# A fused attention and MLP kernel: roots moved ahead of most of a batch's loads, two small loads moved to another queue, and later loads issued earlier in the unit

## Chip, cores, metric

One core of one Trainium2 chip. The metric is the device time of one execution in microseconds (us). Most executions of this kernel lie within 1% of their median; a run over 1.5% above the fastest of the same kernel is marked slow, and only fast runs are compared. In the profile PE is TensorE's matmuls, PEld its weight loads, DVE is VectorE, ACT is ScalarE, POOL is GpSimd and SP is SyncE, which issues hardware DMAs.

## The reference, cut to what matters

```python
# B, H, S, D = 4, 8, 768, 64; 24 chunks of 32 queries; 8 memory rows per head
for c in range(24):                                   # window: 16 left, 32 own, 8 right
    k_full = concat([mem_k, k[:, :, l_start:r_end]])
    v_full = concat([mem_v, v[:, :, l_start:r_end]])
    a = softmax(q_c @ k_full.T / 8)
    attn[:, :, chunk] = a @ v_full
x   = attn.transpose(0, 2, 1, 3).reshape(4, 768, 512)
xn  = (x - mean(x)) / sqrt(var(x) + 1e-6) * g
out = x + relu(xn @ w_ch1) @ w_ch2                    # 512 -> 2048 -> 512, all float32
```

## The kernel before

The 3072 rows of x are 24 tiles of 128 rows. Three tiles make a **unit**; unit u has an up stage (16 groups of four 384-wide products, steps 0 to 15) and a down stage (steps 16 to 27). The attention of the next units, the loads of the next batches and the small work of the other engines are hung on these steps by a hand-made plan: `at(u, step, function, arguments)` emits the function behind that step of unit u. Each engine carries out its list in order.

```python
def load_block(b, blk, which):          # keys or queries of 256 rows, software queue (POOL)
    s = pick(st, ("b", b, blk, which))
    for par in range(2):
        nc.gpsimd.dma_start(out=s[:, 512 * par : 512 * par + 512], in_=dram((k, q)[which], ...))

def load_v(b, g):                       # values of one window pair, software queue (POOL)
    nc.gpsimd.dma_start(out=V[b % 2][lo:hi, g, :, 0:64], in_=dram(v, ...))

def v_mem(b, g0, g1, eng):              # copies the mem values into V, 16 bit, SBUF to SBUF
    copy(eng, V[b % 2][96:W, g0:g1, ...], memv16[96:W, b, ...])

def mix(b, blk, which, eng):            # a raw block to 16-bit layout, SBUF to SBUF
    copy(eng, free(iv_tile, 0, [[64, 2], [128, 8], [1, 64]]), st_tile)

def root(b, t):                         # 1 / sqrt(var) of a tile: two instructions on POOL
    nc.gpsimd.tensor_scalar(out=veps[t % 3], in0=sq[t], ...)
    nc.gpsimd.tensor_tensor(out=rstd[(NT * b + t) % 9], in0=veps[t % 3], in1=mhalf, op=ALU.pow)

def turn_x(b, t):                       # x tile transposed for the up stage
    i = NT * b + t
    if i // 3 >= XU:                    # XU = 2: from unit 2 on a DMA does it
        nc.sync.dma_start_transpose(out=dst, in_=xn[i % 4])
        return
    ...                                 # units 0 and 1: four TensorE transposes, one DVE copy

def finish(t, p):                       # result of a tile; needs the root
    nc.vector.scalar_tensor_tensor(out=o, in0=p, scalar=rstd[t % 9], in1=xs[t % 9],
                                   op0=ALU.mult, op1=ALU.add)
    nc.sync.dma_start(out=out[...], in_=o)
```

The parts of the plan that the change touches (cuts marked with ...):

```python
def attend(i, s0, s1, u):
    ...
    at(u, s1 + (3 if i // 3 < XU else 2), turn_x, b, t)
    at(u, s1 + 2, stats, b, t)                        # sum of squares, ACT
    if i < 6:
        at(1, i % 3, root, b, t)
    else:
        at(i // 3 - 1, 20 + i % 3, root, b, t)
for t in range(3):
    at(0, 13 + t, stats, 0, t)
    at(0, 19 + t, root, 0, t)                         # roots of unit 0
...
order = [(load_pair, (0,))] + [(load_v, (g,)) for g in range(4)]      # batch 1's loads
order += [(load_pair, (1,)), (mem_cols, (pool,)), (load_v, (4,)), (load_v, (5,))]
order += [(load_pair, (2,))] + [(load_v, (g,)) for g in range(6, 12)]
for n, (fn, args) in enumerate(order):
    at(0, 14 + n // 2, fn, *((1,) + args))
...
for b in (2, 3):
    u = 2 * b - 1
    w = u - 1
    for blk in range(3):
        at(w - 1, 23 + blk, load_pair, b, blk)
    at(w, 0, mem_cols, b, pool)
    for g in range(NG):
        at(w, 1 + g // 2, load_v, b, g)
    for i in range(3):
        at(w, 8 + i, v_mem, b, 4 * i, 4 * i + 4, pool)
    for blk in range(3):
        for which in range(2):
            at(w, (3, 9, 18)[blk] + which, mix, b, blk, which, dve)
            at(w, (7, 18, 23)[blk] + 3 * which, cross, b, blk, which)   # DMA transposes
    ...
```

The softmax here doesn't subtract the row's maximum and nothing guards it: scores larger than these inputs give would overflow.

Of the kernel before, what the change touches and what calls it, by code (L numbers as in the profile page):

```python
# [15 lines left out]
def kernel(  # L16
# [12 lines left out]
    nc = tc.nc  # L29
# [53 lines left out]
    turn = {"att": 0, "mm": 0}  # L83
# [6 lines left out]
    def dram(t, offset, pattern):  # L90
        return bass.AP(tensor=t.tensor, offset=offset, ap=[list(p) for p in pattern])

    def free(ap, off, pattern, parts=None):
        p = list(ap.ap[0]) if parts is None else [ap.ap[0][0], parts]
        return bass.AP(tensor=ap.tensor, offset=ap.offset + off, ap=[p] + [list(x) for x in pattern])

    def as16(t):
        return t.bitcast(FP16)

    def copy(eng, out, in_):  # L100
        if eng is nc.scalar:
            eng.copy(out=out, in_=in_)  # L102
        else:
            eng.tensor_copy(out=out, in_=in_)  # L104
# [45 lines left out]
    def mem_keys():  # L150
        p = slot("att")
        pv = as16(p[:, 0, :])
        for half in range(2):
            for par in range(2):
                nc.tensor.matmul(
                    out=pv[64 * par : 64 * par + 64, 128 * half : 128 * half + 128],
                    lhsT=memk16[:, half, :], rhs=identity,
                    is_transpose=True, start=True, stop=True, tile_position=(0, 64 * par),
                )
        for par in range(2):  # L160
            rows = slice(64 * par, 64 * par + 64)
            nc.scalar.copy(
                out=memKT[rows, :, :, :].rearrange("p b j m -> p b (j m)"),
                in_=free(pv[rows, :], 32 * par, [[64, 4], [1, 32]]),
            )
# [31 lines left out]
    def window(b, blk, banks, k0, eng):  # L197

        for half in ((0, 1) if eng is dve else (1, 0)):
            key_piece(b, banks[half], 4 * blk + k0, *PIECES[k0], eng, half)  # L200
# [32 lines left out]

    block_slot = {}

    def quarter_q(b, blk, half, banks):

        for n, eng in ((0, dve), (1, act)):
            copy(eng, free(QR[b % 2], 1024 * blk + 512 * n + 64 * half, [[128, 4], [1, 64]]),
                 free(banks[n], 64 * half, [[128, 4], [1, 64]]))  # L240

    def part_q(b, blk, half, pv, eng):
        copy(eng, free(QR[b % 2], 1024 * blk + 64 * half, [[128, 8], [1, 64]]),
# [181 lines left out]
    def warm(n, m=512, p=None):  # L425
        p = mm[3] if p is None else p
        for _ in range(n):
            nc.tensor.matmul(out=p[:, 0:m], lhsT=zero[:, 0:128], rhs=zero[:, 0:m], start=True, stop=True)


    raws = ((osb[0], osb[1]), (osb[2], xs[4]))
    for which, eng in ((0, nc.sync), (1, nc.scalar)):
        for par in range(2):
            eng.dma_start(
                out=raws[which][par],
                in_=dram((k, q)[which], 4 * par * HS, [[512, 32], [HS, 4], [1, 512]]),
            )
# [3 lines left out]
            out=xs[5 + b][96:W, :], in_=dram(mem_v, b * 4096, [[64, 8], [512, 8], [1, 64]])  # L441
        )

    nc.sync.dma_start(out=memkf, in_=dram(mem_k, 0, [[64, 128], [128 * 64, 2], [1, 64]]))
    nc.sync.dma_start(out=grow, in_=dram(moe_g_ln, 0, [[512, 1], [1, 512]]))
    load_mem_v(0, nc.sync)

    PAIR = 1.0 / 128 + 15.0 / 2**20
# [61 lines left out]
    load_w2(2)  # L510
    load_w2(3)

    warm(6)
    K0 = [as16(mm[0]), as16(mm[1])]
    Q0 = [as16(mm[2]), as16(mm[3])]
    mix_raw(0, raws[0], 0, dve)
    mix_raw(0, raws[0], 1, act)
    mem_keys()
    transpose_block(0, 0, 0, K0)
    mix_raw(1, raws[1], 0, dve)  # L520
    mix_raw(1, raws[1], 1, act)
    window(0, 0, K0, 0, dve)
    window(0, 0, K0, 1, act)
    transpose_block(0, 0, 1, Q0)
    mem_cols(0, dve)
    quarter_q(0, 0, 0, Q0)
    mem_vals(0)
    scores(0, 0)
    soften(0, 0, 0)
    soften(0, 0, 1)  # L530
    window(0, 0, K0, 2, dve)
    p = slot("att")
    nc.tensor.matmul(out=p[:, 0, :], lhsT=gone, rhs=grow, start=True, stop=True)  # L533
    copy(act, gb, p[:, 0, :])
    window(0, 0, K0, 3, act)
    quarter_q(0, 0, 1, Q0)
    mix(0, 1, 0, dve)
    v_mem(0, 0, 2, dve)
    total(cnt[:, 0:1], 16, 128)
    count_v(0, 0, 0)  # L540
    values(0, 0)
    transpose_block(0, 1, 0, K0)
    norm(0, 0)
    window(0, 1, K0, 0, dve)
    key_right(0, 3, dve)
    window(0, 1, K0, 1, act)
    warm(1, 512, mm[2])
    turn_x(0, 0)
    scores(0, 1)
    soften(0, 1, 0)  # L550
    soften(0, 1, 1)
    v_mem(0, 2, 4, dve)
    turn["mm"] = 2
    up_tile(0, 0, 0, act)
    window(0, 1, K0, 2, dve)
    window(0, 1, K0, 3, act)
    key_left(0, 4, dve)
    values(0, 1)
    norm(0, 1)
    warm(1, 512, mm[2])  # L560
    mix(0, 1, 1, dve)
    up_tile(0, 1, 0, act)
    turn_x(0, 1)
    Q1 = [as16(slot("mm")) for _ in range(2)]
    transpose_block(0, 1, 1, Q1)
    quarter_q(0, 1, 0, Q1)
    up_tile(0, 0, 1, act)
    scores(0, 2)
    soften(0, 2, 0)
    soften(0, 2, 1)  # L570
    quarter_q(0, 1, 1, Q1)
    v_mem(0, 4, 6, dve)
    up_tile(0, 1, 1, dve)
    up_tile(0, 2, 0, dve)
# [2 lines left out]
    up_tile(0, 2, 1, act)  # L577
    mix(0, 2, 0, dve)
    up_tile(0, 3, 0, act)
    up_tile(0, 3, 1, dve)  # L580
    turn_x(0, 2)
    mix(0, 2, 1, dve)
    total(cnt[:, 1:2], 0, 80)
    total(cnt[:, 2:3], 96, W)
# [6 lines left out]
    def attend(i, s0, s1, u):  # L591

        b, t = divmod(i, NT)
        at(u, s0, scores, b, t)
        at(u, s0, soften, b, t, 0)
        at(u, s0 + 1, soften, b, t, 1)
        at(u, s1, values, b, t)
        at(u, s1 + 1, norm, b, t)
        at(u, s1 + (3 if i // 3 < XU else 2), turn_x, b, t)
        at(u, s1 + 2, stats, b, t)  # L600
        if i < 6:
            at(1, i % 3, root, b, t)
        else:
            at(i // 3 - 1, 20 + i % 3, root, b, t)

    at(0, 12, turn_keys, 0, 2)
    at(0, 13, more_keys, 0, 2)
    at(0, 14, turn_queries, 0, 2)
    for t in range(3):
        at(0, 13 + t, stats, 0, t)  # L610
        at(0, 19 + t, root, 0, t)
    attend(3, 15, 18, 0)
    at(0, 18, count_v, 0, 1, NG - 1)
    attend(4, 18, 21, 0)
# [13 lines left out]
    order = [(load_pair, (0,))] + [(load_v, (g,)) for g in range(4)]  # L628
    order += [(load_pair, (1,)), (mem_cols, (pool,)), (load_v, (4,)), (load_v, (5,))]
    order += [(load_pair, (2,))] + [(load_v, (g,)) for g in range(6, 12)]  # L630
    for n, (fn, args) in enumerate(order):
        at(0, 14 + n // 2, fn, *((1,) + args))
    at(0, 25, count_v, 1, 0, 0)
# [23 lines left out]
    for b in (2, 3):  # L657
        u = 2 * b - 1
        w = u - 1
        for blk in range(3):  # L660
            at(w - 1, 23 + blk, load_pair, b, blk)
        at(w, 0, mem_cols, b, pool)
        for g in range(NG):
            at(w, 1 + g // 2, load_v, b, g)
        for i in range(3):
            at(w, 8 + i, v_mem, b, 4 * i, 4 * i + 4, pool)
        for blk in range(3):
            for which in range(2):
                at(w, (3, 9, 18)[blk] + which, mix, b, blk, which, dve)
                at(w, (7, 18, 23)[blk] + 3 * which, cross, b, blk, which)  # L670
        at(w, 18, spread, b, 0, dve, act)
        at(w, 27, spread, b, 1, dve, act)
        at(u, 9, spread, b, 2, dve, act)
        attend(6 * b, 2, 7, u)
        attend(6 * b + 1, 7, 13, u)
        attend(6 * b + 2, 13, 18, u)
# [54 lines left out]
```

## Time and profile before

| | before |
|---|---|
| time, median of 3 runs | 231.66 us (230.74 to 231.68) |
| the profiled run | 233.87 us, marked slow; span 232.1 us, mean clock 0.985 |
| PE idle in front of unit 1 | 4.48 + 1.03 us |
| half clock | 6.83 us, from 54.86 on |

The profile that the prediction reads is that of a run 2.2 us above the median, and it was the only one of this kernel. The prediction shows its main lines. The waits of PE complete the picture (who waited for whom; us in total, times, longest): behind the hole in front of unit 1 little is left.

```profile
PE mm L364 <- DVE xT L351: 4.5, 1, 4.5
...
PE mm L364 <- DVE osb L399: 1.0, 1, 1.0
PE mm L364 <- DVE rT L358: 1.0, 1, 1.0
...
PE mm L364 <- DMA xT<-xn: 0.4, 1, 0.4
```

Two lines of the same run's timeline (start, length, engine, operation) become important later. The prediction did not look at them:

```profile
100.21 7.50 POOL L104 COPY V<-memv 8x2560 f16<-8x2560 f16 x3
103.00 2.54 DVE L104 COPY iv<-st 128x1024 f16<-128x1024 f16 x1
```

The same DVE copy takes 0.42 us elsewhere in this trace (at 88.58, 109.00 and others). Beside POOL's copy of the mem values it took 2.54.

### The profile page before, as it was taken

How to read it: one execution, taken by the hardware profiler on the slowest of the kernel's cores; microseconds unless marked ns; L12 is line 12 of the kernel's file. 1: busy time of each engine (PE TensorE's matmuls, PEld its weight loads, DVE VectorE, ACT ScalarE, POOL GpSimd, SP SyncE). 2: the span in 40 equal slices, each digit the busy share in tenths (PEclk: the TensorE clock that was granted, in tenths of full speed). 3: DMA queues.
4: the chain of work that ended last, by engine and by line, in shares of the span. 5: the costliest groups of instructions: out<-in, count | busy, mean ns of one | idle time of the engine just before them, and what ended most of it. 6: DMA issues, size and time to landing. Idle time of an engine off the chain costs nothing.

```text
span 232.1 us, 4947 instructions
## 1 busy us (share of the span) xinstructions
PE 214.6 (92%) x1942; PEld 131.1 (56%) x1942; DVE 134.8 (58%) x324; ACT 103.9 (45%) x219; POOL 111.0 (48%) x172
## 2 busy tenths in 40 slices
PE   4789989955999999999999999997999999999993
PEld 1557985523675557644674466544664566456552
DVE  2867675546486736899685268733674366433221
ACT  2644557620577227742584047702791176104200
POOL 8967755799311668599211965579112002100000
PEclk9999999997699999999999999999999999999999
DMA  6999999999501699998911799999913203211012
GB/s 196 183 198 195 197 192 206 161 158 174 66 3 23 75 190 219 143 150 106 246 32 23 141 212 141 141 110 165 205 24 84 85 15 48 67 47 45 3 45 90
DMA packets 72857, 27.85 MB, mean 120 GB/s; under 512 B 60929, under 2 KB 68865, under 8 KB 72834
## 3 DMA queue, kind: packets, MB, share of 16 engines
q0 software_dynamic: 45632, 14.56, 65.0%
q1 hardware_dynamic: 26914, 12.46, 27.9%
q10 hardware_dynamic: 288, 0.52, 0.8%
q8 instruction: 15, 0.25, 0.5%
q14 instruction: 8, 0.07, 0.1%
HBM read 30.28 MB, written 6.29 MB: 158 GB/s over the span
## 4 chain that ended last, share of the span: by engine, by line
PE 81%; DMA 6%; DVE 4%; POOL 3%; ACT 2%; issue 1%; SPq 1%; DVEq 0%; ACTq 0%
PE mm L364 32%; PE mm L390 29%; PE att L277 6%; PE mm L375 5%; DMA rawk<-iv 5%; PE att L298 4%; DMA memkf<-in_mem_k_dram 2%; PE mm L212 2%; POOL V L128 2%; PE mm L412 2%; PE att L212 1%; POOL st L120 1%; DVE xs L306 1%; PE att L533 1%; POOL rstd L333 1%
## 5 line engine op out<-in xcount | busy, mean ns | idle before, releaser
L364 PE MATMUL mm<-xT,w1c 128*128 128x384 f16 x448 | 80.7, 333 | 7.1 <-DVE xT L351 4.5
L390 PE MATMUL mm<-w2c,rT 128*128 128x512 f16 x368 | 82.6, 379 | 0.0
L364 PEld LDWEIGHTS <-w1c 128*128 128x128 f16 x448 | 49.4, 115 | 31.4 <-issue 9.6
L390 PEld LDWEIGHTS <-rT 128*128 128x128 f16 x368 | 34.9, 98 | 40.0
L358 DVE TENSOR_SCALAR rT<-mm 128x384 f16<-128x384 f32 (+1 forms) x61 | 34.3, 569 | 26.2 <-PE mm L364 22.6
L356 ACT ACTIVATE rT<-mm 128x384 f16<-128x384 f32 (+1 forms) x63 | 31.6, 505 | 37.2 <-PE mm L364 19.2
L128 POOL DMA_DIRECT2D V<-in_v_dram x48 | 39.0, 818 | 16.1 <-DMA V<-in_v_dram 4.0
L287 ACT ACTIVATE AT<-att,band 104x512 f16<-104x512 f32 x48 | 31.4, 686 | 28.5 <-PE att L277 28.5
L399 DVE SCALAR_TENSOR_TENSOR osb<-mm,rstd,xs 128x512 f32<-128x512 f32 x23 | 17.2, 751 | 36.5 <-PE mm L390 29.4
L329 POOL TENSOR_SCALAR veps<-sq 128x1 f32<-128x1 f32 x24 | 5.9, 246 | 61.4 <-ACT junk L323 47.4
L323 ACT ACTIVATE junk<-xs,nmean 128x512 f16<-128x512 f32 x24 | 17.3, 723 | 14.0 <-DVE nmean L312 13.8
L318 DVE SCALAR_TENSOR_TENSOR xn<-xs,nmean,gb 128x512 f16<-128x512 f32 x24 | 20.0, 833 | 0.5
L306 DVE SCALAR_TENSOR_TENSOR xs<-att,rec 128x512 f32<-128x512 f32 x24 | 16.6, 691 | 0.8
L277 PE MATMUL att<-QR,KT 64*104 64x64 f16 x384 | 16.0, 235 | 0.5 <-ACT QR L102 0.5
L333 POOL TENSOR_TENSOR rstd<-veps,mhalf 128x1 f32<-128x1 f32 x24 | 15.4, 641 | 2.0
L102 ACT COPY KT<-rawk 128x352 f16<-128x352 f16 (+1 forms) x12 | 8.9, 801 | 15.7 <-DMA rawk<-iv 15.7
L277 PEld LDWEIGHTS <-KT 64*104 64x104 f16 x384 | 12.7, 134 | 4.2 <-issue 3.4
L104 DVE COPY iv<-st 128x1024 f16<-128x1024 f16 x22 | 13.1, 594 | 2.7 <-DMA QR<-iv 1.8
L104 POOL COPY V<-memv 8x2560 f16<-8x2560 f16 x6 | 14.4, 2434 | 0.1
L375 PE MATMUL mm<-xT,w1c 128*128 128x128 f16 x192 | 13.3, 231 | 0.9 <-DVE xT L351 0.9
L120 POOL DMA_DIRECT2D st<-in_q_dram x22 | 12.3, 579 | 3.4 <-DMA w2c<-in_moe_w_ch_dram 1.7
L120 POOL DMA_DIRECT2D st<-in_k_dram x22 | 12.5, 588 | 2.2 <-DMA st<-in_k_dram 1.3
(70 smaller groups left out, 147.1 us busy)
## 6 DMA issues: line engine op xcount, KB each, us to landing
out_dram<-osb SPq DMA_DIRECT2D x23, 256.0 KB, 3.2
V<-in_v_dram POOLq DMA_DIRECT2D x40, 96.0 KB, 7.9
st<-in_k_dram POOLq DMA_DIRECT2D x22, 128.0 KB, 5.6
st<-in_q_dram POOLq DMA_DIRECT2D x22, 128.0 KB, 6.7
w1c<-in_moe_w_ch_dram POOLq DMA_DIRECT2D x4, 512.0 KB, 9.4
w2c<-in_moe_w_ch_dram POOLq DMA_DIRECT2D x4, 512.0 KB, 9.1
V<-in_v_dram POOLq DMA_DIRECT2D x8, 80.0 KB, 7.7
osb<-in_k_dram SPq DMA_DIRECT2D x2, 256.0 KB, 4.6
```

Source lines behind the costliest of these rows:

```text
L104: eng.tensor_copy(out=out, in_=in_)
L120: nc.gpsimd.dma_start(out=s[:, 512 * par : 512 * par + 512], in_=dram((k, q)[which], (b * H + 4 * par) * HS + blk * 256 * D, [[512, 32], [ ...
L128: nc.gpsimd.dma_start(out=V[b % 2][lo:hi, g, :, 0:64], in_=dram(v, b * H * HS + (64 * g - 16 + lo) * D, [[64, hi - lo], [HS, H], [1, 64]]),)
L277: nc.tensor.matmul(out=p[0:W, par, (4 * gg + j) * 64 : (4 * gg + j) * 64 + 64], lhsT=KT[b % 2][rows, 2 * t + gg, j, :], rhs=free(QR[b % 2] ...
L287: nc.scalar.activation(out=free(AT[t % 3], 32 * c, [[64, 16], [1, 32]]), in_=free(p, 4 * c, [[64, 16], [1, 4], [8, 8]], W), func=ACTF.Exp, ...
L306: nc.vector.scalar_tensor_tensor(out=x.rearrange("p (h d) -> p h d", h=8), in0=free(p, 0, [[128, 8], [1, 64]]), scalar=1.0, in1=free(r, 0, ...
L318: nc.vector.scalar_tensor_tensor(out=xn[i % 4], in0=xs[i % 9], scalar=nmean[t], in1=gb, op0=ALU.add, op1=ALU.mult,)
L356: nc.scalar.activation(out=o, in_=p, func=ACTF.Relu)
L358: nc.vector.tensor_scalar(out=o, in0=p, scalar1=0.0, scalar2=None, op0=ALU.max)
L364: nc.tensor.matmul(out=p, lhsT=free(w1c[c][:, dt, :], i, [[4, 128]]), rhs=xT[u % 2][:, dt, 128 * lo : 128 * (lo + n)], start=(dt == 0), st ...
L375: nc.tensor.matmul(out=p[:, 128 * k_ : 128 * k_ + 128], lhsT=free(w1c[c][:, dt, :], k_, [[4, 128]]), rhs=xT[u % 2][:, dt, 128 * i : 128 * ...
L390: nc.tensor.matmul(out=p, lhsT=rT[c][:, k_, 128 * i : 128 * i + 128], rhs=w2c[c][:, k_, :], start=(c == 0 and k_ == 0), stop=(c == 3 and k ...
```

## The change

Its intent: get the roots out from behind batch 1's loads; get the key halves in first and the mem keys and g out of the way of the prologue; and issue the loads of batches 2 and 3 as soon as a unit's first root is out, so that their data is there earlier. The diff, cut to its core:

```diff
     raws = ((osb[0], osb[1]), (osb[2], xs[4]))
-    for which, eng in ((0, nc.sync), (1, nc.scalar)):
-        for par in range(2):
+    for which in range(2):
+        for par, eng in ((0, nc.sync), (1, nc.scalar)):
             eng.dma_start(out=raws[which][par], ...)
-    nc.sync.dma_start(out=memkf, ...)
-    nc.sync.dma_start(out=grow, ...)
+    nc.gpsimd.dma_start(out=memkf, ...)
+    nc.gpsimd.dma_start(out=grow, ...)
...
-    warm(6)
+    warm(5)
+    p = slot("att")
+    nc.tensor.matmul(out=p[:, 0, :], lhsT=gone, rhs=grow, start=True, stop=True)
     mix_raw(0, raws[0], 0, dve)
     mix_raw(0, raws[0], 1, act)
+    copy(act, gb, p[:, 0, :])
+    transpose_block(0, 0, 0, K0)
     mem_keys()
-    transpose_block(0, 0, 0, K0)
...                                   # the rest of the prologue reordered,
...                                   # whole_q in place of two quarter_q each
         if i < 6:
             at(1, i % 3, root, b, t)
+        elif i % 3 == 0:
+            at(i // 3 - 1, 20, root, b, t)
         else:
-            at(i // 3 - 1, 20 + i % 3, root, b, t)
+            at(i // 3, 7, root, b, t)
...
-        at(0, 19 + t, root, 0, t)
...
+    order[2:2] = [(root0, (t,)) for t in range(3)]
...
-            at(w - 1, 23 + blk, load_pair, b, blk)
+            at(w - 1, 21 + blk, load_pair, b, blk)
...
-            at(w, 1 + g // 2, load_v, b, g)
+            at(w - 1, 24 + g // 4, load_v, b, g)
```

I call its three parts **roots** (the `order[2:2]` line and the one it replaces), **prologue** (everything up to the plan) and **later loads** (the rest).

More of the change, by code (lines that the diff above doesn't have):

```diff
@@ L159, in mem_keys, with memT @@
                 )
+        mem_slot.append(pv)
+    mem_slot = []
+    def memT():
+        pv = mem_slot[0]
         for par in range(2):
@@ L234, with whole_q @@
     block_slot = {}
-    def quarter_q(b, blk, half, banks):
+    def whole_q(b, blk, banks):
         for n, eng in ((0, dve), (1, act)):
-            copy(eng, free(QR[b % 2], 1024 * blk + 512 * n + 64 * half, [[128, 4], [1, 64]]),
-                 free(banks[n], 64 * half, [[128, 4], [1, 64]]))
+            copy(eng, free(QR[b % 2], 1024 * blk + 512 * n, [[1, 512]]),
+                 free(banks[n], 0, [[1, 512]]))
     def part_q(b, blk, half, pv, eng):
@@ L442, in load_mem_v @@
         )
-    nc.sync.dma_start(out=memkf, in_=dram(mem_k, 0, [[64, 128], [128 * 64, 2], [1, 64]]))
-    nc.sync.dma_start(out=grow, in_=dram(moe_g_ln, 0, [[512, 1], [1, 512]]))
+    nc.gpsimd.dma_start(out=memkf, in_=dram(mem_k, 0, [[64, 128], [128 * 64, 2], [1, 64]]))
+    nc.gpsimd.dma_start(out=grow, in_=dram(moe_g_ln, 0, [[512, 1], [1, 512]]))
     load_mem_v(0, nc.sync)
@@ L511 @@
     load_w2(3)
-    warm(6)
     K0 = [as16(mm[0]), as16(mm[1])]
     Q0 = [as16(mm[2]), as16(mm[3])]
+    warm(5)
+    p = slot("att")
+    nc.tensor.matmul(out=p[:, 0, :], lhsT=gone, rhs=grow, start=True, stop=True)
     mix_raw(0, raws[0], 0, dve)
     mix_raw(0, raws[0], 1, act)
+    copy(act, gb, p[:, 0, :])
+    transpose_block(0, 0, 0, K0)
     mem_keys()
-    transpose_block(0, 0, 0, K0)
     mix_raw(1, raws[1], 0, dve)
     mix_raw(1, raws[1], 1, act)
+    transpose_block(0, 0, 1, Q0)
     window(0, 0, K0, 0, dve)
+    memT()
     window(0, 0, K0, 1, act)
-    transpose_block(0, 0, 1, Q0)
     mem_cols(0, dve)
-    quarter_q(0, 0, 0, Q0)
+    whole_q(0, 0, Q0)
+    warm(1, 512, p[:, 1, :])
+    scores(0, 0)
     mem_vals(0)
-    scores(0, 0)
     soften(0, 0, 0)
@@ L531 @@
     window(0, 0, K0, 2, dve)
-    p = slot("att")
-    nc.tensor.matmul(out=p[:, 0, :], lhsT=gone, rhs=grow, start=True, stop=True)
-    copy(act, gb, p[:, 0, :])
     window(0, 0, K0, 3, act)
-    quarter_q(0, 0, 1, Q0)
-    mix(0, 1, 0, dve)
-    v_mem(0, 0, 2, dve)
     total(cnt[:, 0:1], 16, 128)
     count_v(0, 0, 0)
+    mix(0, 1, 0, dve)
+    transpose_block(0, 1, 0, Q0)
+    v_mem(0, 0, 2, dve)
+    window(0, 1, Q0, 0, dve)
+    key_right(0, 3, dve)
     values(0, 0)
-    transpose_block(0, 1, 0, K0)
     norm(0, 0)
-    window(0, 1, K0, 0, dve)
-    key_right(0, 3, dve)
-    window(0, 1, K0, 1, act)
-    warm(1, 512, mm[2])
-    turn_x(0, 0)
     scores(0, 1)
@@ L551 @@
     soften(0, 1, 1)
+    window(0, 1, Q0, 1, act)
     v_mem(0, 2, 4, dve)
-    turn["mm"] = 2
+    turn_x(0, 0)
+    values(0, 1)
+    turn["mm"] = 3
     up_tile(0, 0, 0, act)
-    window(0, 1, K0, 2, dve)
-    window(0, 1, K0, 3, act)
+    norm(0, 1)
+    window(0, 1, Q0, 2, dve)
+    window(0, 1, Q0, 3, act)
     key_left(0, 4, dve)
-    values(0, 1)
-    norm(0, 1)
-    warm(1, 512, mm[2])
+    warm(1, 512, mm[1])
     mix(0, 1, 1, dve)
@@ L565 @@
     transpose_block(0, 1, 1, Q1)
-    quarter_q(0, 1, 0, Q1)
+    whole_q(0, 1, Q1)
     up_tile(0, 0, 1, act)
@@ L570 @@
     soften(0, 2, 1)
-    quarter_q(0, 1, 1, Q1)
     v_mem(0, 4, 6, dve)
@@ L579 @@
     up_tile(0, 3, 0, act)
+    turn_x(0, 2)
     up_tile(0, 3, 1, dve)
-    turn_x(0, 2)
     mix(0, 2, 1, dve)
@@ L602, in attend, with root0 @@
             at(1, i % 3, root, b, t)
-        else:
-            at(i // 3 - 1, 20 + i % 3, root, b, t)
+        elif i % 3 == 0:
+            at(i // 3 - 1, 20, root, b, t)
+        else:
+            at(i // 3, 7, root, b, t)
+    def root0(b, t):
+        root(0, t)
     at(0, 12, turn_keys, 0, 2)
```

## The prediction

> **What bounds the kernel now.** I read the busy-tenths table first, because it says where TensorE is not full.
>
> ```profile
> PE   4789989955999999999999999997999999999993
> POOL 8967755799311668599211965579112002100000
> PEclk9999999997699999999999999999999999999999
> ```
>
> A slice is 5.8 us. PE is full from slice 10 to the end, except slice 27 and the tail; it is short in the first three slices and at slices 8 and 9 (46 to 58 us), where POOL is full. So the kernel is bound by TensorE's own work, and what can be won lies in those holes. The chain that ended last gives PE 81%; the matmuls in it are not touched by the change. The windows show the hole in numbers (columns: stretch, length, busy us of PE, PEld, DVE, ACT, POOL, granted clock, DMA share, GB/s).
>
> ```profile
> 50.00:53.00 3.00, 0.00 (x0) 0.00 (x0) 1.03 (x3) 0.00 (x0) 2.84 (x6) 1.00 1.18 174
> 53.00:57.00 4.00, 1.98 (x14) 1.38 (x14) 2.66 (x6) 0.50 (x2) 3.84 (x6) 0.73 1.51 193
> 54.90:61.70 6.80, 5.77 (x29) 3.35 (x27) 4.04 (x9) 2.73 (x8) 4.88 (x10) 0.50 1.07 131
> 62.00:67.00 5.00, 5.00 (x63) 3.51 (x62) 3.54 (x12) 3.14 (x8) 0.00 (x0) 1.00 0.01 3
> ```
>
> PE does nothing for 3 us, and then has half its clock for 6.8 us, 5.77 of them busy. The timeline of that hole tells the cause.
>
> ```profile
> 48.30 1.10 POOL L120 DMA_DIRECT2D st<-in_q_dram x2
> ...
> 49.73 0.57 POOL L333 TENSOR_TENSOR rstd<-veps,mhalf 128x1 f32<-128x1 f32 x1
> 50.27 1.64 POOL L128 DMA_DIRECT2D V<-in_v_dram x2
> 50.34 0.75 DVE L399 SCALAR_TENSOR_TENSOR osb<-mm,rstd,xs 128x512 f32<-128x512 f32 x1 [2.18 <-POOL rstd L333]
> ...
> 52.86 0.75 DVE L399 SCALAR_TENSOR_TENSOR osb<-mm,rstd,xs 128x512 f32<-128x512 f32 x1 [1.63 <-POOL rstd L333]
> 53.52 0.41 DVE L351 COPY xT<-att 128x512 f16<-128x512 f16 x1
> ...
> 53.99 0.81 PE L364 MATMUL mm<-xT,w1c 128*128 128x384 f16 x4 [4.48 <-DVE xT L351]
> ```
>
> POOL issues DMAs and computes the roots (rstd) in one order. The roots of tiles 0 to 2 stand behind batch 1's loads; their inputs, the sums of squares, were done on ACT by 36.7 us, but the first root ended at 50.3, the second at 52.8, the third at 55.7. DVE, in order too, waited 5.1 us in all for them in front of the copy of xT that PE needed. PE lost 4.48 us there, and 1.03 us more behind the third root.
>
> The rest of PE's waits: 3.1 us at 7 us for the mem keys (transposed ahead of the first key block), 0.9 us at 29.4 for an xT copy, and 0.4 and 1.0 us at 158 and 162. In the prologue the line
>
> ```profile
> PE att L155 <- DVE memk L104: 3.1, 1, 3.1
> ```
>
> stands first in the waits of PE up to 36 us.
>
> **What the Trainium skill says.** (1) "TensorE: Matmul & The Clock Gate", Part 1: the PE clock falls to half after an idle window of about 3.4 us and comes back after a sustained busy one. The trace agrees: 4.48 us idle, then 6.83 us at clock 0.50. It also says that a cold start runs at half. The clock row shows 1.00 there, yet 16 score matmuls take 0.90 us at 9.9 us and 0.65 at 23.4, so I read the first 21 us as cold. (2) The same page, "Architectural detail": GpSimd, ACT and DVE are strict FIFO, and PE lets only weight loads go ahead. That is the mechanism of the hole. (3) "DMA: Bandwidth & Descriptors", "Queues, rings and completion order": each DMA engine goes round the queues that have work. The trace agrees: a 128x512 transpose landed in 2.4 to 3.1 us beside an idle software queue, and in 7.9 us (issued at 93.06) beside POOL's values loads.
>
> **The change part by part.**
>
> *Roots of unit 0 early.* They now stand on POOL right behind batch 1's first four block loads and its first values load, which POOL issued by 36.8 us. Three roots take 3 x 0.85 = 2.5 us, so they are done by about 39.5, and unit 0's last results are wanted at about 47 to 49. The three waits of DVE go. What stays is DVE's own work between the last down product and the next unit: two results and the xT copy, so PE's gap falls from 4.48 to about 0.2, and the 1.03 goes. Gain 5.5 us. The clock no longer drops: 5.77 us of busy PE at half clock shrink by half, 2.9 us. But DVE becomes the limit for some 5 us there (results 0.75 each, v_mem 0.82, four key copies 1.0, relus 0.56 each against 0.65 us for four 384-wide products). I walked its order against the four PSUM buffers and find three short waits, 0.6 us together. Net 5.5 + 2.9 - 0.6 = **7.8 us**. POOL loses 2.5 us at 37 to 39.5, but it sat idle for 1.0 and 2.4 us between 37.6 and 41.8 waiting for slots, and loads then still took 4 to 8 us to land, so the DMA queue does not run dry.
>
> *Prologue.* The two key halves now go first on two queues, so both land at about 4.8 us (before: 4.6 and 6.06), and the mem keys stand behind the first transposes. The keys' transposes start at about 6, not 7.4. g's product (2.07 us, ahead of the values at 12.8 and holding them 0.6 us) moves into the dead time at 3.5 to 6. That is worth some 0.5 to 1 us at the first scores; values and scores of tile 1 also go ahead of the first up tile, so tile 1's transposes come at about 19.7 in place of 21.42. Little of that survives, though. POOL's loads land back to back at 190 to 200 GB/s until 47 us, and the change gives the stream the same bytes in the same order. DVE already waited for it:
>
> ```profile
> 31.08 0.43 DVE L104 COPY iv<-st 128x1024 f16<-128x1024 f16 x1 [0.89 <-DMA st<-in_q_dram]
> ```
>
> That load landed at 30.99 and will again, within 0.3. From there DVE still has copy 0.43, sums 0.45, key copies 0.56, relu 0.69, key copies 0.54, edges 0.24: it ends at about 33.9, and scores of tile 3 start there, against 34.80. So the prologue brings **1.0 us**, not 2.6, and PE shows 1 to 2 us of waiting between 28 and 33 us.
>
> *Loads of batches 2 and 3 behind the unit's first root.* Today they wait for the third tile's root (78.79 us and 128.90 us). Behind the first (70.1 and 121.3) they start 7.6 to 8.7 us earlier in the unit. For batch 3 this clears the stretch from 145 to 166 us, where a transpose rawk<-iv took 10.45 us and PE waited 0.38 and 1.02 us. Gain **1.3 us** of these 1.4. The price is that they now run beside the last x transpose of units 1 and 3. In the old clock it is issued at 79.24 and 128.30, behind a 256 KB result on the same queue, and wanted at 85.3 and 133.2, 6.0 and 4.9 us later. Loaded, I put it at 6.5 us on average (between 3 and 7.9): waits of about 0.5 and 1.5 us, **2.0 us lost**.
>
> *Other parts.* Whole instead of half query copies remove four small copies (0.28 to 0.40 us each) that were not on the path that sets the end; one zero product fewer is 0.4 us in dead time. Counted as nothing.
>
> Sum: 231.66 - 7.8 - 1.0 - 1.3 + 2.0 = **223.6 us**.
>
> **Rivals.** *A: the wait is only replaced.* With the roots gone, DVE (2.66 of 4.0 us busy in the hole) or the block loads for batch 1 could hold PE instead. Against it: the keys for unit 1 landed at 42.1 and its queries at 43.4, well ahead of 48. Then only half of the 7.8 would come: about 227.5. *B: the earlier loads collide.* If each loaded transpose takes 9 us (8.86 us was the worst of x, issued 149.20, wanted at 157.7), the waits are 3 and 4 us: about 228.5. A wait above 3.4 us would also cost clock again. For it speaks the 8.6 us of rawk at 89 us; against it, that at 79 us the loads are the wide block loads, not yet all values. *C: no collision, and a prologue that keeps its gain* because g's product warms the clock early: 231.66 - 7.8 - 2.6 - 1.3 = 220.0. *D: nothing moves* because the hole was off the path: ruled out nearly, since PE is full from 57 us to the end, so that what it starts earlier it ends earlier.
>
> **Range and chances.** The 7.8 is measured idle and clock, good to 1.5 us; the prologue to 1; the collisions to 2.5. Range 220.5 to 227.0. Faster by over 2% means below 227.0; only A or B in full reach above: 0.89 faster, 0.10 same, 0.01 slower.
>
> **What would show it.** Right: no half clock after the first 21 us; rstd of tiles 0 to 2 done by 41 us; PE's gap before unit 1's first product under 1 us; block loads for batch 2 issued some 8 us before the unit's end result, and the last rawk transposes of batch 3 faster than 10 us. Unit 1's first product at about 48.7 us (now 53.99). Wrong, if PE waits over 1 us for DVE at 48 to 54 (A), if PE waits over 3 us for xT at the start of units 2 or 4 (B), if scores of tile 3 come before 33 us (the stream was not the limit), or if g lands so late that its product holds the first transposes beyond 7 us.

## The result, and the profile after

| | before | after |
|---|---|---|
| time, median | 231.67 us (230.74 to 232.07, 4 runs) | 240.81 us (238.75 to 243.16, 4 runs) |
| ratio of fast runs | 1 | 1.0371, 95% interval 1.0293 to 1.045 |
| profiled span, mean clock | 232.1 us, 0.985 | 239.5 us, 0.979 |

A ratio here is the mean time of one kernel's fast runs over that of the other's of the same rounds, so not quite the ratio of the medians. The changed kernel is 3.7% slower; 223.6 us had been predicted. It computes the right result.

In the busy-tenths table of the kernel after (a slice is 6.0 us), the hole at slices 8 and 9 is gone, as predicted. There are two new ones, at slices 13 and 22, and half clock behind each and once more at slice 26:

```profile
PE   3769978998999599899999599799999999999994
...
POOL 7955865898296589620056799720011101200000
PEclk9999999999999979999999979979999999999999
```

The waits of PE in the kernel after say whom it now waits for: x transposes, 3.0 and 2.7 us (5.7 in two), and relus of DVE in front of the down stages.

```profile
PE mm L370 <- DMA xT<-xn: 5.7, 2, 3.0
PE att L523 <- DMA grow<-in_moe_g_ln_dram: 3.7, 1, 3.7
PE mm L396 <- DVE rT L364: 2.0, 2, 1.0
...
PE att L304 <- DVE xs L312: 1.0, 2, 0.8
```

Where the time goes is best read from the start of each stage in the timelines, that is from the first product of the up (U) and down (D) stage of each unit, in us. The profiled runs of the experiments with the roots alone and without the later loads (below) stand beside it.

| stage | before | after | after minus before | roots alone | after without later loads | what the later loads cost |
|---|---|---|---|---|---|---|
| U1 | 54.0 | 52.8 | -1.2 | 50.1 | 52.6 | 0.2 |
| D1 | 73.2 | 69.3 | -3.9 | 66.4 | 69.2 | 0.1 |
| U2 | 85.3 | 84.2 | -1.1 | 78.4 | 81.7 | 2.5 |
| D2 | 99.0 | 100.6 | +1.6 | 92.1 | 95.4 | 5.2 |
| U3 | 109.3 | 111.0 | +1.7 | 102.5 | 105.8 | 5.2 |
| U4 | 133.4 | 137.9 | +4.5 | 126.6 | 129.9 | 8.0 |
| D4 | 147.1 | 155.0 | +7.9 | 140.3 | 143.6 | 11.4 |
| U5 | 158.1 | 167.1 | +9.0 | 151.7 | 154.5 | 12.6 |
| end | 232.1 | 239.5 | +7.4 | 224.6 | 227.1 | 12.4 |

The gain of the roots is there until D1. From there on the later loads take 2.5 + 2.7 us at units 2 and 2.8 + 3.4 + 1.2 at units 4 and 5. The timeline of the kernel after at the first place:

```profile
77.83 3.40 PE L396 MATMUL mm<-w2c,rT 128*128 128x512 f16 x15
...
84.25 1.44 PE L370 MATMUL mm<-xT,w1c 128*128 128x384 f16 x4 [3.02 <-DMA xT<-xn]
...
90.33 7.66 POOL L104 COPY V<-memv 8x2560 f16<-8x2560 f16 x3
...
93.88 1.94 DVE L104 COPY iv<-st 128x1024 f16<-128x1024 f16 x1
...
96.20 2.08 DVE L104 COPY iv<-st 128x1024 f16<-128x1024 f16 x1
...
100.61 3.61 PE L396 MATMUL mm<-w2c,rT 128*128 128x512 f16 x16 [1.00 <-DVE rT L364]
```

Two things happen in a row. The x transpose of tile 8 was issued at 75.39 and PE got it at 84.25, about 8.8 us later (its landing is not in the record), beside the loads that POOL issued from 66.22 on. The first four products then take 1.44 us where 0.81 is usual: half clock. Behind that, POOL's copies of the mem values, which now come at 90.33 and not at 100.21, hold up two raw copies of DVE, the relus behind them are late, and PE waits 1.00 us more. The windows of the kernel after give the clock (length, busy us of PE, PEld, DVE, ACT, POOL, clock, DMA share, GB/s):

```profile
84.00:87.40 3.40, 3.15 (x23) 1.66 (x24) 0.56 (x1) 0.69 (x1) 3.03 (x5) 0.50 2.05 213
87.40:95.00 7.60, 7.60 (x88) 5.19 (x86) 5.68 (x12) 4.99 (x10) 7.20 (x8) 1.00 1.44 124
...
155.70:159.10 3.40, 3.40 (x10) 1.17 (x9) 2.63 (x7) 2.21 (x4) 1.25 (x2) 0.50 0.42 82
```

There are three such stretches of 3.41 us (from 84.0, 138.6 and 155.7); with PE busy throughout, each costs about half its length, 1.7 us. Their number differs from run to run: the three fast runs of the changed kernel have mean clocks of 0.979, 0.986 and 0.993, which fits three, two and one of them.

The traces also show when such a stretch begins. Within a run the stretches begin whole multiples of 3.41 us apart (here 54.6 and 17.1 us, 16 and 5 times 3.41), as if the clock were decided anew at each step of a grid, which lies differently in each run. In all traces of this case together, eleven stretches began at full clock between the cold start and the tail. In the step of 3.41 us in front of each, PE had been idle for 1.79 to 2.79 us in total, in one gap or in several. Steps with at most 1.44 us of idling brought none; the one step between, 1.94 us from 48.04 on in the kernel before, did not either. So what counts is the idling within a step, not the length of one gap, and where a gap falls on the grid is luck.

### The profile page after: what moved, and what is told of

Its sections match the earlier page's. It is cut to its first block, busy times and chain, and to the rows that moved or that the text cites. A ratio compares the mean times of both kernels' runs of the same rounds, so it can differ in the third digit from the quotient of the medians.

```text
span 239.5 us, 4956 instructions
## 1 busy us (share of the span) xinstructions
PE 216.8 (91%) x1941; PEld 132.3 (55%) x1941; DVE 134.4 (56%) x322; ACT 103.7 (43%) x217; POOL 110.7 (46%) x174
## 3 DMA queue, kind: packets, MB, share of 16 engines
HBM read 30.28 MB, written 6.29 MB: 153 GB/s over the span
## 4 chain that ended last, share of the span: by engine, by line
PE 60%; DMA 22%; DVE 7%; POOL 5%; issue 4%; ACT 0%; DVEq 0%; POOLq 0%
PE mm L370 27%; PE mm L396 24%; DMA w2c<-in_moe_w_ch_dram 8%; DMA xT<-xn 7%; DMA w1c<-in_moe_w_ch_dram 5%; PE att L283 4%; DVE iv L104 2%; PE att L304 2%; DMA st<-in_q_dram 2%; POOL V L128 2%; POOL st L120 2%; PE mm L418 1%; DVE rT L364 1%; DVE xn L324 1%; DVE xs L312 1%
## 5 line engine op out<-in xcount | busy, mean ns | idle before, releaser
L396 PE MATMUL mm<-w2c,rT 128*128 128x512 f16 x368 | 84.3, 385 | 2.0 <-DVE rT L364 2.0
L396 PEld LDWEIGHTS <-rT 128*128 128x128 f16 x368 | 35.5, 99 | 43.2 <-issue 4.2
L362 ACT ACTIVATE rT<-mm 128x384 f16<-128x384 f32 (+1 forms) x63 | 31.1, 501 | 44.8 <-PE mm L370 25.4
L128 POOL DMA_DIRECT2D V<-in_v_dram x48 | 37.3, 787 | 11.9 <-DMA w1c<-in_moe_w_ch_dram 3.1
L324 DVE SCALAR_TENSOR_TENSOR xn<-xs,nmean,gb 128x512 f16<-128x512 f32 x24 | 18.7, 778 | 0.5
L104 DVE COPY iv<-st 128x1024 f16<-128x1024 f16 x22 | 16.4, 747 | 2.6 <-DMA st<-in_q_dram 2.5
L339 POOL TENSOR_TENSOR rstd<-veps,mhalf 128x1 f32<-128x1 f32 x24 | 14.5, 604 | 2.0
L104 POOL COPY V<-memv 8x2560 f16<-8x2560 f16 x6 | 15.2, 2563 | 0.1
L120 POOL DMA_DIRECT2D st<-in_q_dram x22 | 12.4, 587 | 3.6 <-DMA w2c<-in_moe_w_ch_dram 2.0
L120 POOL DMA_DIRECT2D st<-in_k_dram x22 | 13.2, 652 | 1.5 <-DMA w1c<-in_moe_w_ch_dram 1.4
L304 PEld LDWEIGHTS <-AT 104*64 104x64 f16 x384 | 8.8, 114 | 9.3 <-issue 5.6
```

Source lines behind the costliest of these rows:

```text
L104: eng.tensor_copy(out=out, in_=in_)
L324: nc.vector.scalar_tensor_tensor(out=xn[i % 4], in0=xs[i % 9], scalar=nmean[t], in1=gb, op0=ALU.add, op1=ALU.mult,)
L362: nc.scalar.activation(out=o, in_=p, func=ACTF.Relu)
L396: nc.tensor.matmul(out=p, lhsT=rT[c][:, k_, 128 * i : 128 * i + 128], rhs=w2c[c][:, k_, :], start=(c == 0 and k_ == 0), stop=(c == 3 and k ...
```

## The experiments

### One part at a time: roots, later loads, prologue, and all but the later loads

These four ran in one call; before took 231.61 us there (median of 10 runs).

**e1_roots**: the kernel before with the roots alone.

```diff
-        at(0, 19 + t, root, 0, t)
...
+    order[2:2] = [(root0, (t,)) for t in range(3)]
```

> The kernel before with one part of the change alone: the three roots of unit 0 stand behind batch 1's first values load. My theory (the change is the sum of three parts, and the roots are a gain): about 225 us (223 to 227), PE's gap before unit 1's first product under 1 us, no half clock after 21 us. Rival (the roots only trade one wait for another, as the gain that the changed kernel shows by unit 1's down products, 3.9 us ahead, is all there is): 228 us or more.

Measured: 226.03 us (225.6 to 226.37), ratio 0.975 (0.9713 to 0.9786): 5.6 us gained. The windows at the old hole, to be held against those of before in the prediction, show PE at work and the clock at full:

```profile
50.00:53.00 3.00, 2.46 (x25) 1.93 (x25) 2.94 (x7) 0.99 (x3) 3.00 (x5) 1.00 1.24 219
53.00:57.00 4.00, 3.82 (x35) 2.49 (x35) 2.65 (x8) 2.80 (x7) 3.51 (x8) 1.00 1.93 221
```

PE's gap before unit 1 is 0.54 us and no half clock follows. The mechanism is right, so rival A falls: nothing else holds PE there. The gain, though, lies halfway between the 7.8 us of the prediction and the 3.9 us of A.

**e2_loads**: the kernel before with the later loads alone.

```diff
-            at(i // 3 - 1, 20 + i % 3, root, b, t)
+            at(*((i // 3, 7) if i % 3 else (i // 3 - 1, 20)), root, b, t)
-            at(w - 1, 23 + blk, load_pair, b, blk)
+            at(w - 1, 21 + blk, load_pair, b, blk)
-            at(w, 1 + g // 2, load_v, b, g)
+            at(w - 1, 24 + g // 4, load_v, b, g)
```

> The kernel before with one part alone: the loads of batches 2 and 3 behind the unit's first root, and the other two roots of a unit after them. My theory now, from the trace after: the loads run beside the last x transposes of units 1 and 3, PE waits some 3 us at the start of units 2 and 4, and the clock halves after each: 8 to 11 us slower than before, 240 to 243 us. Rival (the waits come from the prologue's shift of the DMA stream, and the loads alone are harmless): 230 to 233 us.

Measured: 243.83 us (243.37 to 244.19), ratio 1.0518 (1.0479 to 1.0556): 12.2 us lost. By themselves, too, the later loads cost far more than the 2.0 us (less 1.3 gained) of the prediction. The trace has the same signs as the changed kernel's: PE waits 1.95 and 2.62 us in front of units 2 and 4 (the profile puts the first down to a result of DVE, the second to the transpose), 1.00 and 1.90 us for relus in front of their down stages, and two new stretches of half clock (from 102.71 and 157.32).

**e3_prologue**: the kernel before with the prologue alone, made from the changed kernel by undoing the other two parts.

```diff
-    order[2:2] = [(root0, (t,)) for t in range(3)]
+        at(0, 19 + t, root, 0, t)
...                                   # and the later loads as in the kernel before
```

> The kernel before with the prologue part alone (mem keys and g first on POOL's queue, g's product behind the zero products, the reordered first two tiles). My theory: g lands at about 7 us and holds the first transposes, and POOL's stream starts later, so that unit 0's first down product comes some 2 us later than before (35.4 us): 233 to 235 us. Rival (the stream has slack, and the hole at 49 us swallows the delay): 231 to 232 us.

Measured: 233.77 us (232.86 to 234.74, 7 runs), ratio 1.0084 (1.0055 to 1.0113): 2.2 us lost where 1.0 should have been gained.

**e4_no_loads**: the changed kernel with the later loads as in the kernel before (the second diff above, turned round).

> The changed kernel with the later loads and roots put back where they were before: prologue and unit 0's roots alone. My theory (parts add): 227 to 229 us, that is the roots' gain less 2 us of prologue, and the waits on xT at the start of units 2 and 4 are gone. Rival (the waits on xT are the early arrival of PE, not the loads): it still waits 2 to 3 us there and takes 232 us or more.

Measured: 228.11 us (227.57 to 228.9), ratio 0.9833 (0.9791 to 0.9875). The parts add up: 231.6 - 5.6 + 2.2 + 12.2 = 240.4 us, against 240.81 measured; and this kernel, 228.11, has 231.6 - 5.6 + 2.2 = 228.2. Two things need an explanation: the 12.2 us and the 2.2 us.

### The prologue: which of its loads is to blame

Two theories stood against each other. **S**: POOL, which carries out its list in order, now has two small DMA issues ahead of everything else, so its whole stream of loads starts later. **G**: g lands late, and its product stands in front of the first transposes on PE. The timeline of POOL before:

```profile
1.93 0.74 POOL L452 MEMSET V<- 104x768 f32 x1
2.61 1.68 POOL L128 DMA_DIRECT2D V<-in_v_dram  x2
```

And after:

```profile
1.26 0.91 POOL L450 DMA_DIRECT2D memkf<-in_mem_k_dram  x1 [0.82 <-POOLq L725]
2.17 0.53 POOL L451 DMA_DIRECT2D grow<-in_moe_g_ln_dram  x1
...
4.59 1.51 POOL L128 DMA_DIRECT2D V<-in_v_dram  x2
```

The first load of values is issued 1.98 us later.

**e5_hw** (e4_no_loads with the two small loads back on SP):

```diff
-    nc.gpsimd.dma_start(out=memkf, ...)
-    nc.gpsimd.dma_start(out=grow, ...)
+    nc.sync.dma_start(out=memkf, ...)
+    nc.sync.dma_start(out=grow, ...)
```

> Roots and prologue without the later loads (228.1 us in the run before), but mem keys and g are loaded on SP's queue behind a key and a query half, as before the change. Theory S (the prologue's 2 us are the later start of POOL's stream of loads, whose block 2 queries landed 3 us later): the stream is back, those queries land at about 31 us, and the time is about 226 us or less. Theory G (they are g's product, which holds the first transposes until g has landed): g still lands at 6.5 us or later, so about 228 us.

**e6_glate** (e4_no_loads with g's product and its copy back behind the scores of tile 0):

```diff
-    p = slot("att")
-    nc.tensor.matmul(out=p[:, 0, :], lhsT=gone, rhs=grow, start=True, stop=True)
...
-    copy(act, gb, p[:, 0, :])
...
-    warm(1, 512, p[:, 1, :])
...
     window(0, 0, K0, 2, dve)
+    p = slot("att")
+    nc.tensor.matmul(out=p[:, 0, :], lhsT=gone, rhs=grow, start=True, stop=True)
+    copy(act, gb, p[:, 0, :])
```

> Roots and prologue without the later loads, but g's product and its copy stand behind the scores of tile 0, as before the change; mem keys and g still go first on POOL's queue; the zero product ahead of the scores is left out. Theory G: the first transposes start at about 6 us in place of 9.2, and the time is about 226 us. Theory S: the first transposes start early, but the queries of block 2 still land at about 34 us and the time stays at about 228 us.

Measured in one call (before 231.3 us, 29 runs): e5_hw 225.36 us (224.61 to 225.99), ratio 0.9749 (0.9683 to 0.9815); e6_glate 228.24 us (226.89 to 230.75, 18 runs), ratio 0.9858 (0.9831 to 0.9885). The queue decides, S holds: putting the two loads back on SP is worth about 1.1% against e6_glate in the same call (0.8% against e4_no_loads, which ran in another call; there the intervals overlap slightly), that is 2 to 3 us. Moving g's product brings nothing that can be measured. DVE's wait for the queries of block 2 shows the stream. In the kernel after:

```profile
34.10 0.44 DVE L104 COPY iv<-st 128x1024 f16<-128x1024 f16 x1 [2.49 <-DMA st<-in_q_dram]
```

With the two loads on SP:

```profile
31.00 0.43 DVE L104 COPY iv<-st 128x1024 f16<-128x1024 f16 x1 [1.26 <-DMA st<-in_q_dram]
```

With g's product late instead:

```profile
33.86 0.43 DVE L104 COPY iv<-st 128x1024 f16<-128x1024 f16 x1 [3.78 <-DMA st<-in_q_dram]
```

In the kernel before, the same copy started at 31.08. The stream's start moved by 2.0 us, that load by 3.0, and PE's gap with g in front (3.73 us in the kernel after) was dead time anyway: in e6_glate PE gets its first transposes at 6.29 and scores of tile 0 at 9.9, and is still as late as e4_no_loads at 37 us, because it then waits for the stream.

### The later loads: transposes by DMA, and POOL's copies

Two costs could make up the 12.2 us: the DMA transposes of the last x tile of units 2 and 4 (tiles 8 and 14), which run beside the loads; and POOL's copies of the mem values, which run beside DVE's raw copies. Each was taken away alone, then both.

**e7_pe_x** (the changed kernel, tiles 8 and 14 turned by TensorE):

```diff
-        if i // 3 >= XU:
+        if i // 3 >= XU and i not in (8, 14):
...
-        at(u, s1 + (3 if i // 3 < XU else 2), turn_x, b, t)
+        at(u, s1 + (3 if i // 3 < XU or i in (8, 14) else 2), turn_x, b, t)
```

> The changed kernel whole, but tiles 8 and 14 (the last of units 2 and 4) are transposed by TensorE and copied by DVE in place of the DMA transpose. My theory (the later loads cost time first through the DMA transposes that they slow): PE's waits of 3.0 and 2.65 us at the start of units 2 and 4 go, and with them the half clock behind each; TensorE has 0.8 us more to do: 240.8 less 6 to 8 us, 233 to 235 us. What stays is the slow DVE copies beside POOL's mem-value copies. Rival (the loads hold PE in another way, for example by tiles 6, 7, 12 and 13 landing as late): less than 3 us gained, 238 us or more.

**e8_vmem_dve** (the changed kernel, the mem values of batches 2 and 3 copied by DVE):

```diff
-            at(w, 8 + i, v_mem, b, 4 * i, 4 * i + 4, pool)
+            at(w, 8 + i, v_mem, b, 4 * i, 4 * i + 4, dve)
```

> The changed kernel whole, but the mem-value copies of batches 2 and 3 are done by DVE, not POOL. Theory (POOL's copies, now 10 us earlier in the unit, run beside DVE's copies of the raw blocks and slow them from 0.42 to 2 us): those copies return to about 0.42 us, PE's waits of 1.0 us for a relu ahead of the down products of units 2 and 4 go, and the half clock behind the second: 236.5 to 239 us. Rival (the slow copies come from POOL issuing loads): the copies stay at 2 us, 240 us or more.

Measured in the call of e5_hw: e7_pe_x 230.71 us (228.48 to 236.89, 12 runs), ratio 0.9971 (0.9936 to 1.0006): 9.3 us of the loss by the ratios, 10.1 by the medians of the two calls, are gone with the two transposes, more than the 6 to 8 expected. In its eight fast runs the clock is 0.999 to 1.0, so all three stretches of half clock are gone and not only two. Its four slow runs show 0.985 to 0.992, which fits one or two stretches; the mean of all twelve is 231.5 us. e8_vmem_dve 235.14 us (233.28 to 238.04; three fast runs), ratio 1.0215 (1.0115 to 1.0315): 3.6 us below the changed kernel by the ratios, 5.7 by the medians. The two intervals overlap a little, so this size is rough.

By the ratios the two gains add up to 12.9 us, against a loss of 12.5 us by the same measure; by the medians they would overlap, and these runs do not decide it. In e8_vmem_dve the transposes are still late, PE's waits say so:

```profile
PE mm L370 <- DMA xT<-xn: 4.2, 2, 2.1
```

but the raw copies are quick again, though they stand right behind DVE's own copies of the mem values:

```profile
91.25 1.56 DVE L104 COPY V<-memv 8x2560 f16<-8x2560 f16 x2
92.84 0.43 DVE L104 COPY iv<-st 128x1024 f16<-128x1024 f16 x1
...
94.62 0.43 DVE L104 COPY iv<-st 128x1024 f16<-128x1024 f16 x1
```

The profiled run of e8_vmem_dve has no half clock behind its two waits for a transpose, by luck of the grid: the gap of 2.06 us fell into two steps as 1.44 and 0.62 us, that of 2.15 us as 1.41 and 0.74. In e12_blocks_only below, a gap of 2.05 us fell almost whole into one step and half clock followed. So part of what this run gained is not owed to its edit.

In e7_pe_x POOL still makes these copies, and DVE's are still slow (the profiled run is one of the slow state, 232.79 us; only the lengths are read from it):

```profile
88.67 7.53 POOL L104 COPY V<-memv 8x2560 f16<-8x2560 f16 x3
89.65 1.91 DVE L104 COPY iv<-st 128x1024 f16<-128x1024 f16 x1
91.94 2.08 DVE L104 COPY iv<-st 128x1024 f16<-128x1024 f16 x1
```

So the slow copy goes with POOL's, not with the loads. The Trainium skill, "SBUF — State Buffer", section "Who interferes with whom", has the reason: DVE and GpSimd share a pair of ports, and a DVE copy in a mode that takes both pairs and a GpSimd operation exclude each other for the length of a whole instruction. The trace of the changed kernel agrees: in its timeline from 95 us on, the last two of POOL's copies start at 92.75 and take 5.24 us, so they end at about 95.4 and 98.0; DVE's two copies end at 95.82 and 98.28, that is 0.4 and 0.3 us behind them, while such a copy alone takes 0.42. DVE waited for the running POOL copy and then did its own. The lines of before at 100.21 and 103.00 show the same thing.

**e9_both** (e7_pe_x and e8_vmem_dve together):

> The changed kernel with both mends at once: the last x tiles of units 2 and 4 (tiles 8 and 14) turned by TensorE, and the mem values of batches 2 and 3 copied into V by DVE in place of POOL. If these two collisions are all that the early loads cost, and the early loads bring nothing, it stands at the time of the changed kernel without early loads, 227.5 to 229 (228.1 measured). If the early loads also bring the 1.3 us of my prediction (batch 3's transposes clear), 226 to 227. If a third cost exists that neither mend touches, over 229.5. No gap of PE over 1 us behind 40 us and no half clock are expected in the first two cases.

Measured (before 231.82 us, 13 runs, in the call of e9 to e12): 229.72 us (228.95 to 230.6, 10 runs), ratio 0.9922 (0.9894 to 0.9951). No half clock is left behind the cold start (all ten runs have a clock of 0.997 or more) and no wait for a transpose: of the 12.2 us some 10 to 11 are explained by the two collisions. It lies above 229.5, so in the third of the cases that I had set out: a cost that neither mend touches. Its ratio is about 0.9% (2.1 us) above that of e4_no_loads, which ran in another call. Its trace has a wait of 0.78 us for DVE's relus in front of each of D2 and D4, where DVE now has POOL's copies to do, and the two tiles' transposes are now TensorE's own work (0.39 us for four matmuls in the timeline of e1_roots). That is 2 x 0.78 + 2 x 0.39 = 2.3 us, an estimate from these traces. It fits, but the profiled runs end at 227.4 and 227.1 us, and no run separates these remains.

**e12_blocks_only** (the changed kernel, only the blocks of keys and queries early):

```diff
-            at(w - 1, 24 + g // 4, load_v, b, g)
+            at(w, 1 + g // 2, load_v, b, g)
```

> The changed kernel with only the block loads early; the values loads of batches 2 and 3 put back behind the first steps of the even unit. Theory: the x transposes of tiles 8 and 14 run beside the block loads, but with the values loads away fewer descriptors compete in their last part, and POOL's v_mem still stands where it stood. If block loads alone slow the transposes and move the raw copies to where POOL copies mem values: 237 to 241. If the values loads (rows of 256 bytes) are what slows them: 229 to 233.

Measured: 239.0 us (238.8 to 239.64), ratio 1.0313 (1.0273 to 1.0353), hardly below the changed kernel's 1.0371 (the intervals overlap). The blocks alone do nearly all of it. PE's waits and the timeline of DVE and POOL show both collisions again:

```profile
PE mm L370 <- DMA xT<-xn: 5.1, 2, 3.0
...
PE mm L396 <- DVE rT L364: 1.5, 2, 0.8
```

```profile
88.40 7.51 POOL L104 COPY V<-memv 8x2560 f16<-8x2560 f16 x3
...
94.11 2.08 DVE L104 COPY iv<-st 128x1024 f16<-128x1024 f16 x1
```

The transpose of tile 14 was issued at 128.64 and landed at 136.90, 8.26 us.

### Is there a version that beats both kernels?

**e10_hw_glate** (the edits of e5_hw and e6_glate together):

> The kernel without early loads, mem keys and g on the hardware queue, and g's product put back behind the scores of tile 0. Alone the first brought 228.1 to 225.4, the second nothing measurable (228.2). If g's product never held the path, 225.0 to 225.8 again. If with the stream out of the way the product is what bounds the prologue, below 224.8.

**e11_all_mended** (the whole change, with the edits of e9_both and of e5_hw):

> The whole change with the three mends: both of the first run here and mem keys and g on the hardware queue. If the costs add, it is 2.7 us below the first run of this call, so about 225.4 if early loads bring nothing and 224 to 224.5 if they bring 1.3 us. It would then be the version that beats both kernels.

Measured: e10_hw_glate 226.69 us (225.82 to 227.28), ratio 0.9775 (0.9729 to 0.982); e11_all_mended 226.53 us (226.24 to 226.93), ratio 0.9772 (0.9735 to 0.9809). With e1_roots (0.975) and e5_hw (0.9749) these four cannot be told apart. All beat the kernel before by 2.2 to 2.5% (only for e1_roots does the whole interval lie beyond 2%), and the roots alone do it. e10_hw_glate lies above both of the times that were expected of it; it shows no gain from a late product. Mended, the prologue and the later loads neither cost nor bring anything that these runs can show. e11_all_mended expected 225.4 for early loads that bring nothing and 224 to 224.5 for loads that bring 1.3 us; it reached neither. Against e9_both in the same call it is 1.5% (3.2 us) faster, so the queue's gain shows once more.

## Why the prediction was wrong

**The roots: mechanism right, size read from a slow run.** Its main signs appeared: in the kernel after PE's gap before unit 1 is 0.48 us, and the 6.83 us of half clock behind it are gone. The roots of tiles 0 to 2 run from 39.64 to 42.3 us (41 was said), and unit 1 starts at 52.79 (50.12 with the roots alone) where 48.7 was said. The term was 7.8 us. Trace against trace the roots alone bring 3.9 us at U1, 6.8 at D1 and 7.5 at the end, so the working holds within 1 us; but timed they bring 5.6 us (and 5.7 with the changed prologue: 233.77 - 228.11). The profiled run of before was 2.2 us slower than its timed runs. I read its whole hole as if it stood in every run and did not hold it against the median. Where those 2.2 us lay in the profiled run is not recorded, but the half clock is a likely part. In e3_prologue, whose profiled run is a fast one, the same hole (4.50 us) is followed by the same 6.83 us of half clock; 2.06 us of them fall into the hole itself, where they cost nothing, and U1 to D1 takes 17.8 us in place of 19.2. And of the 48 fast timed runs of before in the experiments, the 16 with the profiled run's clock of 0.985 average 232.0 us, the 17 with 0.989 to 0.993 average 230.8. A small slip adds to it: the 5.5 us count the whole of 4.48 + 1.03, though 0.2 was to stay.

**The prologue: a step failed.** "The change gives the stream the same bytes in the same order", so the load that landed at 30.99 "will again, within 0.3". It landed at 34.01. The bytes of the stream were the same; its start was not, since I counted the mem keys and g as loads on a faster or slower queue and not as 0.91 and 0.53 us of work on POOL in front of it, which also began 0.54 us later. I had even named the stream as the limit, which is why nothing else in the prologue could repay it: +2.2 in place of -1.0 us. That g's product might hold the first transposes was watched for (7.22 us in the kernel after, so beyond the 7 that was set as a sign), but e6_glate shows that it cost nothing. With the stream back in place the rest of the working holds: in e5_hw scores of tile 3 start at 33.88, as the predicted 33.9, and not at 36.98 as in the kernel after. One reading was off, without consequence: the loads move 190 to 200 GB/s only until 40 us, 163 to 164 from there to 47.

**The later loads: the step that decided.** "Loaded, I put it at 6.5 us on average ... waits of about 0.5 and 1.5 us, 2.0 us lost." The transposes took about 8.8 and 7.91 us, and PE waited 3.02 and 2.65 us. That is nearly rival B (3 and 4 us). B too would have been far off with its 228.5, because it stopped at the waits. From them to the 12.4 us of the table above there are three more terms:

- Half clock: 3 x 1.7 = 5.1 us in the profiled run (the other two fast runs had one and two stretches). The prediction's threshold, that only a wait above 3.4 us costs clock, was taken from the skill. In these runs gaps of 3.02, 2.65 and 2.05 us were followed by half clock, and the third stretch, from 155.7 on, came behind the two short gaps around D4, 0.79 and 1.00 us within one step of the grid.
- DVE held by POOL's copies: PE waits of 1.00 us before D2, and of 0.79 and 1.00 us around D4. The prediction did not have this term at all, although the trace of before showed it (2.54 us at 103.00). It spoke of what earlier loads collide with, not of what POOL would do once it had them out of its way: its mem copies came 10 us earlier and met two raw copies.
- Against that, e4_no_loads itself waits 0.60 us for one of the transposes.

Sum: 3.02 + 2.65 + 5.1 + 2.79 - 0.6 = 13.0, against 12.4 in the traces.

**The gain from batch 3's clear transposes: seen, but worth nothing.** The loaded transpose at 150.48 (10.45 us before) takes 3.08 us in the kernel after, as said. But the PE waits it was to remove (0.38 and 1.02 us) are already nearly gone without it: with early roots and no early loads PE waits 0.32 us there in e4_no_loads, 0.58 in e5_hw and 0.87 in e1_roots.

**The sum and the chances.** Predicted -7.8 - 1.0 - 1.3 + 2.0 = -8.1; measured -5.6 + 2.2 + 12.2 = +8.8, with no gain to set apart. 0.01 for slower was far too little. The range let the collisions vary by 2.5 us, but they were linked with two further mechanisms, the clock and the shared port, that made them dearer.

**What stays open.** How a DMA transpose loses time beside block loads (what share of it is arbitration, what share the 256 KB result ahead of it on the same queue) was not taken apart. Why the step with 1.94 us of idling brought no half clock, and 1.79 us did elsewhere, is open too, and so are the 2 us or so between e9_both and e4_no_loads.

## What to carry to other kernels

Before moving loads forward, list everything that will be in flight or be released then: a DMA transpose with 5 to 6 us of slack is not hidden beside a stream of block loads, and an engine that is rid of its loads earlier starts its next work earlier, beside something else. Two small loads put first on the engine that issues the main stream delayed that stream by 2.0 us here, so look for another queue for such loads. A gap of PE can cost more than its length: here 1.8 us of idling within 3.41 us was enough for half clock. And compare the profiled run's time with the median before a hole in it is counted in full.

## What the Trainium skill lacked or had wrong

- "TensorE: Matmul & The Clock Gate", Part 1 gives an idle window of about 3.4 us, which runs freely, for the drop to half clock. That the half clock comes in pieces of 3.41 us on a grid that differs from run to run agrees. What the page lacks is how much of a window has to be idle: here 1.79 us was enough (0.79 + 1.00 us in front of 155.7 in the kernel after), while gaps of 2.06 and 2.15 us that lay across two windows (e8_vmem_dve) brought none. Read as a limit that a single gap has to exceed, as the prediction did, it misled.
- "DMA: Bandwidth & Descriptors", "Queues, rings and completion order" says that the queues take turns, but not what a DMA transpose loses by it: 2.4 to 3.1 us beside an idle software queue, 7.91, 8.26 and about 8.8 us beside the loads of a batch.
- "SBUF — State Buffer" was right on the shared ports, and the runs put a number on it: a 128x1024 16-bit copy on DVE went from 0.42 to between 1.91 and 2.54 us beside a copy on POOL. The prediction should have drawn on it.
